# Low halves of four paired feed-forward chunks: subtracted on VectorE instead of loaded from DRAM, with a new list of order shifts

## The chip, the cores and the metric

The kernel runs on one core of a Trainium2 chip. The core has five engines that the profile names: PE (TensorE, matmul; PEld is its weight load), DVE (VectorE), ACT (ScalarE), POOL (GpSimd) and SP (SyncE, which issues nearly all DMAs here). Each engine works through its own list of instructions in order; semaphores tie the lists together. The metric is the device time of one execution in microseconds (us), as a median of several runs.

## What is computed

A transformer block on x of 2048 rows by 640 columns: layer norm, attention with 32 heads of 20 over a window of 8 keys spaced by 2, output product and residual; then layer norm and a SwiGLU feed-forward of width 1728, and residual.

```python
def _B_ref(x, w_gate, w_up, w_down):
    g = _silu(x @ w_gate)
    u = x @ w_up
    return (g * u) @ w_down

x = A_x
h = x + _A_ref(_layernorm(x, axis=-1), A_wqkv, A_wo)
h2 = h + _B_ref(_layernorm(h, axis=-1), B_w_gate, B_w_up, B_w_down)
return h2
```

All inputs and the output are float32.

## The kernel before

**Three passes for one product.** TensorE gets its operands in a reduced format (`F32R`). Each float32 operand is split into a high half (a cast, on ScalarE) and a low half (the float32 value minus the high half, a subtraction on VectorE). A product is the sum of three passes: high weights by high rows, high weights by low rows, low weights by high rows. The low half of a weight is thus wanted by the last pass only.

**Blocks and chunks.** The 2048 rows are four blocks `b` of 512. The feed-forward's width is cut into 14 chunks `i` of 128 (the last has 64). A chunk's weights are one row of `in_ffn`: 1280 columns of gate and up, 640 of down. Blocks 0 and 1 run all chunks in `ffn`. Blocks 2 and 3 share their chunks 0 to 11 in six pairs (p, p+6) by a scheme that saves one of eight products. Its first part, `early(p)` (L1074), runs chunk p with block 2 alone: two of the five column groups first, whose sums go to DRAM as `msc`, then the other three, the gate, and the first 320 columns of down. The later part is `pair(p)` (L1177). Chunks 12 and 13 run in `plain`. "The third block" is block 2; "its last four paired chunks" are `early(2)` to `early(5)`.

**How a chunk's weights come in.** `load_ffn` (L933) loads the raw chunk into one of two raw buffers in turn (L939), has ScalarE cast gate and up (L940) and down (L941) to the high halves, and then gets the low halves in one of two ways. With block 0 VectorE subtracts them (`split`, L957, in pieces of 640 columns) and SP stores them in DRAM, as `lsc`. With blocks 1 and 2 (`LOADED`, L26) SP loads them from `lsc` (L945): gate and up in one load, down in another. Chunks take turns in two buffers for gate and up (`GU`) and three for down (`DN`), so a low half can be written once the chunk two (three) back has been multiplied.

**What runs beside it.** While TensorE works on chunks 0 to 5 of block 2, the kernel also finishes attention for block 3, multiplies by `wo` for block 3 (L891) and normalises its rows, and forms combinations of down weights (`down_combinations`, L1117: loads L1121, subtractions L1124, casts L1131, low halves L1132, stores L1134 to `tsc`). When these are through, `column_combinations` (L1137) forms sums of the columns of blocks 2 and 3 (L1148 to L1165), which `pair` multiplies. The additions of L1115 move the first products of down out of four banks.

**What sets the order.** `Plan.add` notes each operation with its engine, a cost and what it reads and writes; the dependencies follow from that. `Plan.order` runs a planner over the whole list several times, with costs and due times, and gets a start for each operation. To it is added a shift from `SHIFT`, a table from the operation's number to microseconds. The program is then written in order of these sums, as far as the dependencies allow, and that order is each engine's order. `SHIFT` has 318 entries, over the whole length of the kernel. The engines' waits are put in by the dependencies, whatever the order.

Of the kernel before, what the change touches and what calls it, by code (L numbers as in the profile page):

```python
# [10 lines left out]
F32 = mybir.dt.float32  # L11
# [13 lines left out]
KEPT = range(NF)  # L25
LOADED = (1, 2)  # L26
TURN = (1,)
# [10 lines left out]
PR = {'tp': 6, 'mx': 2, 'mh': 2, 'ml': 2, 'mld': 3, 'dt': 2.2, 'g1': 0.6, 'y1': 0.6, 'x': 0.5, 'yst': 8, 'yld': 2, 'wqd': 4, 'wqh': 0.5, 'wql': 4, 'qev': 1, 'kvs': 0.4, 'atl': 1.2, 'exp': 0.5, 'ost': 3, 'wod': 2, 'woh': 8, 'wol': 1.2, 'old': 1.5, 'fld': 4, 'lst': 6, 'wev': 1.5, 'fh': 2.2, 'fl': 8, 'ln1': 8, 't1': 1, 'wo0': 1.2, 'wo': 2.2, 'ln1t': 1.2, 'xb': 0.4, 'tr': 10, 't1t': 2.2, 'ln1d': 0.5, 'hst': 10, 'hld': 10, 'ht': 1, 'hc': 2, 'jd': 3, 'jp': 8, 'js': 4, 'jl': 0.4, 'ja': 0.5, 'jfld': 1.2, 'jfh': 4, 'jfl': 1, 'jhi': 4, 'jmu': 0.4, 'jlo': 0.9, 'jcm': 0.5, 'w3': 1, 'w3e': 8, 'w3o': 0.4, 'w3x': 8, 'w3l': 2.2, 'jy': 6}  # L38

SHIFT = {  # L40
# [190 lines left out]
def program(tc, x_in, wqkv_in, wo_in, ffn_in, ffl_in, const_in, out):  # L231
# [7 lines left out]
    with tc.tile_pool(name="sb", bufs=1) as sb, tc.tile_pool(  # L239
# [89 lines left out]
        def rf(o, n):  # L329
            return ("fa", o, o + n)  # L330
# [4 lines left out]
        def rr(o, n):  # L335
            return ("ra", o, o + n)
# [596 lines left out]
        def load_ffn(b, i, gu, dn, m=640):  # L933
# [9 lines left out]
            if b in LOADED and i in KEPT:  # L943
                for o, at_, m in parts:
                    P.add("SP", 0.45, lambda o=o, at_=at_, m=m: Q.dma_start(r_(at_, m).bitcast(F32), lsc[i, :, o : o + m]), r=[(f"L{i}", o, o + m)], w=[rr(at_, m)], prio=PR["fld"], nbytes=nb(128, 4 * m))  # L945
                return
# [3 lines left out]
            split("DVE", dn[1], raw + n, dn[0], 640, 64 if last else 0)  # L950
# [3 lines left out]
        def split(eng, lo, raw, hi, n, p0):  # L954
            E, c = (V, tt(640)) if eng == "DVE" else (G, 1.8)
            for o in range(0, n, 640):
                P.add(eng, c, lambda o=o: E.tensor_sub(ra[p0:, lo + o : lo + o + 640], fa[p0:, raw + o : raw + o + 640], ra[p0:, hi + o : hi + o + 640].bitcast(F32)),  # L957
                      r=[rf(raw + o, 640), rr(hi + o, 640)], w=[rr(lo + o, 640)], prio=PR["fl"])
# [99 lines left out]
        def plain(i, x, xr):  # L1058
# [4 lines left out]
            load_ffn(2, i, gu, dn)  # L1063
# [10 lines left out]
        def early(p):  # L1074
# [4 lines left out]
            load_ffn(2, p, gu, dn, 320)  # L1079
# [442 lines left out]
```

## Time and profile before

| what | value |
| --- | --- |
| time, median of 3 runs | 838.03 us (836.65 to 838.71) |
| the profiled execution: time | 839.46 us |
| the profiled execution: span | 837.3 us |
| granted TensorE clock, mean | 0.998 |
| instructions: TensorE matmuls | 4061 |
| instructions: VectorE | 916 |
| moved by DMA | 211.08 MB |

The span runs from the first to the last instruction; the time holds a little more. A share of busy time is a mean over stages: on TensorE the kernel begins with the products for q, k and v (up to about 240 us) and goes on with the feed-forward of blocks 0 and 1 (to about 550 us), then chunks 12 and 13 and the early chunks of block 2 (to about 645 us), then the pairs, and from about 771 us the last down products. VectorE works on attention from the first stage until about 570 us. A row of the waits reads: engine and place, what it waited for, us in total, times, longest. A row of groups reads: line, engine, operation, what is written from what, shapes, count, then busy us, mean ns, and idle time before. A row of the chain or the timeline begins with the start and the length in us; SPq marks SP's queue of DMA issues.

### The profile page before, as it was taken

How to read it: one execution, taken by the hardware profiler on the slowest of the kernel's cores; microseconds unless marked ns; L12 is line 12 of the kernel's file. 1: busy time of each engine (PE TensorE's matmuls, PEld its weight loads, DVE VectorE, ACT ScalarE, POOL GpSimd, SP SyncE). 2: the span in 40 equal slices, each digit the busy share in tenths (PEclk: the TensorE clock that was granted, in tenths of full speed). 3: DMA queues.
4: the chain of work that ended last, by engine and by line, in shares of the span. 5: the costliest groups of instructions: out<-in, count | busy, mean ns of one | idle time of the engine just before them, and what ended most of it. 6: DMA issues, size and time to landing. Idle time of an engine off the chain costs nothing.

```text
span 837.3 us, 11299 instructions
## 1 busy us (share of the span) xinstructions
PE 827.1 (99%) x4061; PEld 713.5 (85%) x4061; DVE 756.1 (90%) x916; ACT 421.0 (50%) x740; POOL 23.1 (3%) x34
## 2 busy tenths in 40 slices
PE   8999999999999999999999999999999999999997
PEld 6888888889978888887888988888888888888997
DVE  7599999999999999999999999998869888777982
ACT  7856463333682435754543386565695333323440
POOL 0000000000100000001000000000000000000000
PEclk9999999999999999999999999999999999999999
DMA  8896968568679665899899668889999634357721
GB/s 274 296 363 253 284 200 275 199 201 307 185 217 351 242 192 194 313 308 352 281 319 350 250 188 317 260 267 315 375 348 312 227 115 150 128 182 250 269 105 68
DMA packets 113223, 211.08 MB, mean 252 GB/s; under 512 B 37952, under 2 KB 70400, under 8 KB 112528
## 3 DMA queue, kind: packets, MB, share of 16 engines
q1 hardware_dynamic: 113008, 210.12, 74.1%
q8 instruction: 32, 0.52, 0.3%
q10 hardware_dynamic: 160, 0.25, 0.1%
q14 instruction: 23, 0.19, 0.1%
HBM read 151.27 MB, written 59.05 MB: 251 GB/s over the span
## 4 chain that ended last, share of the span: by engine, by line
PE 86%; DVE 7%; DMA 3%; issue 2%; ACT 0%; SPq 0%; DVEq 0%; ACTq 0%
PE bank L963 22%; PE bank L644 20%; PE bank L1047 16%; PE bank L974 11%; PE bank L1299 7%; PE bank L891 4%; PE bank L1069 2%; DVE fa L693 1%; DVE fa L700 1%; DMA tsc<-acts 1%; DMA ra<-lsc 1%; PE bank L1094 1%; DVE fa L736 1%; PE bank L1104 1%; DMA fa<-in_ffn_dram 1%
## 5 line engine op out<-in xcount | busy, mean ns | idle before, releaser
L963 PE MATMUL bank<-shb,ra 128*128 128x512 f32 x810 | 190.0, 390 | 1.2 <-DVE shb L508 1.2
L963 PEld LDWEIGHTS bank<-shb,ra 128*128 128x128 f32 x810 | 151.4, 188 | 32.7 <-ACT shb L507 1.4
L644 PE MATMUL bank<-ra,sha 128*128 128x480 f32 x480 | 105.0, 379 | 0.0
L644 PE MATMUL bank<-ra,shb 128*128 128x480 f32 x470 | 102.5, 378 | 0.0
L644 PEld LDWEIGHTS bank<-ra,sha 128*128 128x128 f32 x480 | 90.2, 188 | 13.6
L644 PEld LDWEIGHTS bank<-ra,shb 128*128 128x128 f32 x470 | 88.1, 188 | 13.2
L693 DVE TENSOR_TENSOR fa<-fa 128x2560 f32<-128x2560 f32 x32 | 90.3, 2821 | 0.9 <-DMA fa<-ksc 0.2
L728 DVE TENSOR_TENSOR fa<-fa 128x2560 f32<-128x2560 f32 x32 | 90.3, 2823 | 0.8
L1047 PE MATMUL bank<-shb,ra 128*128 128x512 f32 x360 | 89.7, 395 | 0.7 <-DVE fa L991 0.6
L700 DVE TENSOR_REDUCE fa<-fa 128x128 f32<-128x2560 f32 x32 | 90.0, 2813 | 0.4
L974 PE MATMUL bank<-ra,acts 128*128 128x512 f32 x328 | 80.7, 391 | 0.0
L1047 PEld LDWEIGHTS bank<-shb,ra 128*128 128x128 f32 x360 | 65.8, 188 | 16.8 <-DVE fa L1224 1.7
L736 DVE TENSOR_TENSOR fa<-fa 128x1280 f32<-128x1280 f32 (+2 forms) x70 | 76.8, 1097 | 1.3
L649 ACT ACTIVATE st<-bank,fa 128x480 f32<-128x480 f32 x64 | 41.1, 656 | 69.7 <-PE bank L644 65.3
L891 PE MATMUL bank<-ra 128*128 128x320 f32 x480 | 74.4, 310 | 0.7 <-ACT ra L808 0.6
L891 PEld LDWEIGHTS bank<-ra 128*128 128x128 f32 x480 | 71.7, 188 | 3.7 <-ACT fa L894 1.6
L974 PEld LDWEIGHTS bank<-ra,acts 128*128 128x128 f32 x328 | 61.2, 188 | 13.2 <-DVE acts L998 0.5
L1047 PE MATMUL bank<-ra 128*128 128x512 f32 x288 | 69.1, 390 | 0.0
L1047 PEld LDWEIGHTS bank<-ra 128*128 128x128 f32 x288 | 53.9, 188 | 11.2
L1224 DVE TENSOR_TENSOR fa<-bank,fa 128x512 f32<-128x512 f32 x60 | 41.1, 690 | 19.9 <-PE bank L1047 19.1
L940 ACT CAST ra<-fa 128x1280 fp32r<-128x1280 f32 (+1 forms) x38 | 45.6, 1206 | 24.2 <-PE bank L963 12.3
L997 ACT CAST acts<-fa 128x512 fp32r<-128x512 f32 x34 | 21.0, 619 | 47.6 <-DVE fa L987 45.9
(189 smaller groups left out, 1061.8 us busy)
## 6 DMA issues: line engine op xcount, KB each, us to landing
fa<-in_ffn_dram SPq DMA_DIRECT2D x28, 960.0 KB, 6.7
fa<-ksc SPq DMA_DIRECT2D x16, 880.0 KB, 5.1
fa<-vsc SPq DMA_DIRECT2D x16, 880.0 KB, 7.6
ra<-lsc SPq DMA_DIRECT2D x21, 640.0 KB, 6.1
ra<-lsc SPq DMA_DIRECT2D x27, 320.0 KB, 3.6
lsc<-ra SPq DMA_DIRECT2D x13, 640.0 KB, 4.7
fa<-in_ffn_dram SPq DMA_DIRECT2D x12, 640.0 KB, 3.9
ra<-tsc SPq DMA_DIRECT2D x8, 960.0 KB, 7.3
```

The source lines that it names most:

```text
L644: T.matmul(banks[bk][:, 0:480], l, r_(wq(g, w, c), 480), start=(p, c) == first_mm, stop=(p, c) == last_mm)
L649: P.add("ACT", act(480) + 0.06, lambda bk=bk, j=j: A.activation(stage_t()[:, so : so + 1920].rearrange("p (t j c) -> p t j c", t=3, j=NJ)[ ...
L693: P.add("DVE", dve(2560), lambda: V.tensor_tensor(f(PROD, 2560).rearrange("p (j w c) -> p j w c", j=2, w=W), window(ko, 2 * jp), f(qo + 32 ...
L700: P.add("DVE", dve(2560), lambda: V.tensor_reduce(f(lo + 128 * jp, 128), f(PROD, 2560).rearrange("p (n d) -> p n d", d=DH), axis=AX.X, op= ...
L728: V.tensor_tensor(f(PROD, 2560).rearrange("p (j w d) -> p j w d", j=2, d=DH), bass.AP(tensor=fa[:, vo : vo + 160].tensor, offset=fa[:, vo ...
L736: V.tensor_add(dst(v), v[:, :, 0:m, :], v[:, :, m : 2 * m, :])
L891: T.matmul(banks[bk][:, 0:320], l, r_(m, 320), start=p == 0 and c == 0, stop=p == 2 and c == NC - 1)
L940: P.add("ACT", act(n), lambda: A.copy(r_(gu, n), f(raw, n)), r=[rf(raw, n)], w=[rr(gu, n)], prio=PR["fh"])
L963: T.matmul(banks[bk], r_(gu + 1280 * w + wid * c + col, 128), x2(a, c), start=p == 0 and c == 0, stop=p == 2 and c == NC - 1)
L974: T.matmul(banks[bk][:, lo:hi], l, m, start=first and p == 0, stop=last and p == len(passes) - 1)
L1047: T.matmul(banks[bk], r_(ws[w] + 256 * q, 128), x(a, c), start=start and p == n == q == 0, stop=stop and p == 2 and n == len(terms) - 1 an ...
L1299: T.matmul(banks[bks[j]][:, 0:320], t(a, 128, 128 * j), r_(ws[w], 320), start=p == q == 0, stop=p == NP - 1 and q == 2)
```

## The change

Two names are new: `MADE_EARLY`, the paired chunks whose low halves are made, and `MADE_LAST`, the same for the last chunks with block 3, which is empty. `load_ffn` takes a flag `made`, and with it goes the way of block 0, subtraction on VectorE, but stores nothing. `split` is made to take widths under 640, since an early chunk has 320 columns of down. So `early(2)` to `early(5)` lose two loads each from `lsc` (1280 and 320 columns) and gain three subtractions each (640, 640 and 320 columns). Since each such chunk has one operation more, the numbers of all later operations move up by one to four. The table `SHIFT` is replaced as a whole: 220 entries for 318, and of the operations in the one 58 are in the other too. One of the new entries names a new operation (1893, the second subtraction of chunk 2).

```diff
+MADE_EARLY = (2, 3, 4, 5)
+MADE_LAST = ()
...
-    7: 3.5, 9: -106.8, 22: 0.4, 31: -515.8, 32: -221.5, 33: -238.8, 34: -84.5, 35: -34.6, 36: -483.8, 37:
...
+    8: 4.6, 9: -130.2, 14: 2, 18: 1.5, 21: 1.1, 29: -118.6, 33: -131.6, 34: -30.4, 35: -16.7, 36: -93.7, 37:
...
+    1856: -25.6, 1857: -71.3, 1868: 1, 1872: 8.2, 1874: 2.3, 1877: 7, 1878: -75, 1879: -127.1, 1881: -31.3,
+    1882: -100.7, 1883: -151.9, 1884: -53.5, 1893: 20.6, 1898: -4.7, 1903: -0.9, 1918: 2, 1923: -54.8, 1931:
...
-        def load_ffn(b, i, gu, dn, m=640):
+        def load_ffn(b, i, gu, dn, m=640, made=False):
...
-            if b in LOADED and i in KEPT:
+            if b in LOADED and i in KEPT and not made:
                 for o, at_, m in parts:
                     P.add("SP", 0.45, lambda o=o, at_=at_, m=m: Q.dma_start(r_(at_, m).bitcast(F32), lsc[i, :, o : o + m]), r=[(f"L{i}", o, o + m)], w=[rr(at_, m)], prio=PR["fld"], nbytes=nb(128, 4 * m))
                 return
             split("DVE", gu + 1280, raw, gu, n, 0)
...
-            split("DVE", dn[1], raw + n, dn[0], 640, 64 if last else 0)
+            split("DVE", dn[1], raw + n, dn[0], m, 64 if last else 0)
...
         def split(eng, lo, raw, hi, n, p0):
-            E, c = (V, tt(640)) if eng == "DVE" else (G, 1.8)
+            E, k = V if eng == "DVE" else G, min(n, 640)
             for o in range(0, n, 640):
-                P.add(eng, c, lambda o=o: E.tensor_sub(ra[p0:, lo + o : lo + o + 640], fa[p0:, raw + o : raw + o + 640], ra[p0:, hi + o : hi + o + 640].bitcast(F32)),
-                      r=[rf(raw + o, 640), rr(hi + o, 640)], w=[rr(lo + o, 640)], prio=PR["fl"])
+                P.add(eng, tt(k) if eng == "DVE" else 1.8, lambda o=o: E.tensor_sub(ra[p0:, lo + o : lo + o + k], fa[p0:, raw + o : raw + o + k], ra[p0:, hi + o : hi + o + k].bitcast(F32)),
+                      r=[rf(raw + o, k), rr(hi + o, k)], w=[rr(lo + o, k)], prio=PR["fl"])
...
-            load_ffn(2, i, gu, dn)
+            load_ffn(2, i, gu, dn, made=x is not x2 and i in MADE_LAST)
...
-            load_ffn(2, p, gu, dn, 320)
+            load_ffn(2, p, gu, dn, 320, p in MADE_EARLY)
```

55 rows, old and new, of the table SHIFT are left out of this document.

## The prediction

> **What bounds the kernel now.** I read the page first, then the windows by stage, TensorE's waits, the stretch around the paired chunks in windows of 10 us, and the queues there.
>
> ```profile
> span 837.3 us, 11299 instructions
> ...
> PE 827.1 (99%) x4061; PEld 713.5 (85%) x4061; DVE 756.1 (90%) x916; ACT 421.0 (50%) x740; POOL 23.1 (3%) x34
> ```
>
> The profiled execution took 839.46 us, 2.16 beside its span; the median, 838.03, lies 1.43 below it. So a span S stands for a median of S + 2.16 - 1.43 = S + 0.73. TensorE is busy for all but 10.2 us of the span, and the change takes no matmul away. It can win only idle time of TensorE; these windows and waits say where that is.
>
> ```profile
> 60.00:120.00 60.00, 60.00 (x280) 52.15 (x279) 59.28 (x46) 40.38 (x82) 3.44 (x4) 1.00 0.78 255
> ...
> 180.00:240.00 60.00, 58.78 (x316) 53.27 (x315) 59.40 (x58) 34.72 (x74) 3.90 (x4) 1.00 0.70 224
> ...
> 563.00:618.00 55.00, 53.55 (x310) 47.54 (x309) 43.83 (x88) 35.77 (x66) 0.00 (x0) 1.00 0.96 343
> ...
> 760.00:838.00 78.00, 72.94 (x475) 71.02 (x473) 55.12 (x96) 26.26 (x44) 0.00 (x0) 1.00 0.46 162
> ```
>
> ```profile
> PE bank L605 <- DVE sha L608: 1.8, 1, 1.8
> PE bank L555 <- POOL ra L1401: 1.3, 1, 1.3
> PE bank L963 <- DVE shb L508: 1.2, 1, 1.2
> PE bank L891 <- ACT ra L808: 0.6, 1, 0.6
> PE bank L1047 <- DVE fa L991: 0.6, 1, 0.6
> PE bank L891 <- ACT fa L894: 0.2, 1, 0.2
> PE bank L1047 <- ACT fa L986: 0.2, 1, 0.2
> ```
>
> The columns of a window are its length, then busy time of PE, PEld, DVE, ACT and POOL, clock, DMA share and GB/s. Of the 10.2 us, 4.4 lie behind the last matmul (77.3 us from 760 to the span's end, less 72.94) and 3.1 in the two waits of the first microseconds, L555 and L605. What is left in the middle is 1.2 in 180 to 240 and 1.45 in 563 to 618, the stretch where the DMA engines are busy for 96% and where the paired chunks begin: 2.7 us in all. Those four parts make 10.2, so everywhere else TensorE runs without a break.
>
> **The change, removed.** Each of four chunks loses one load of 640 KB and one of 160 KB from the store of low halves.
>
> ```profile
> ra<-lsc SPq DMA_DIRECT2D x21, 640.0 KB, 6.1
> ...
> ra<-lsc SPq DMA_DIRECT2D x6, 160.0 KB, 4.8
> ```
>
> ```profile
> 579.23 1.07 SPq L945 DMA_DIRECT2D ra<-lsc  x2
> ...
> 630.49 0.49 SPq L945 DMA_DIRECT2D ra<-lsc  x1
> ```
>
> ```profile
>   PEld bank L1047: 0.2, 1
> ```
>
> Between the first and the last of these two issues stand nine loads; eight go (the ninth is chunk 1's down half). That is 4 x 800 KB = 3.28 MB, at the 343 GB/s of the stretch 9.6 us of full DMA. But of all low-half loads between 560 and 660 us TensorE's side waited for one, and for 0.2 us (the last row). The gain can come only by way of other transfers that run faster:
>
> ```profile
> 582.36 9.78 DMA tsc<-acts
> ...
> 593.72 1.29 DVE fa L1124 x3
> ...
> 607.12 2.12 PE bank L1047 x8
> ```
>
> In the chain the store of turned weights takes 9.78 us in the saturated stretch; its buffer, then ScalarE's and VectorE's work behind it, lead to the waits for L894 and L986 (0.15 each; rounded to 0.2 in their rows). With the first three of the removed loads gone from 579 to 591 us, these 0.3 us can go. The waits for L991 and L808 (1.15 together) end before the first removed load is issued: only the order can mend them. I take half of them, 0.6, with 0 and 1.15 as ends. Removal and order in this stretch: -0.9 (ends 0 and -1.45).
>
> **Added.** Per chunk two subtractions of 640 columns and one of 320, as in L957 (same form) and L1124 (320 columns):
>
> ```profile
> L957 DVE TENSOR_TENSOR ra<-fa,ra 128x640 fp32r<-128x640 f32 x40 | 31.8, 819 | 0.0
> ...
> L1124 DVE TENSOR_TENSOR fa<-fa 128x320 f32<-128x320 f32 x24 | 11.1, 488 | 1.9 <-DMA fa<-in_ffn_dram 1.6
> ```
>
> 8 x 0.819 + 4 x 0.488 = 8.5 us of VectorE. Back to back they overlap a little: in the chain above three L1124 take 1.29, 0.43 each instead of 0.488; 12 x 0.06 less gives 7.8. [...] I keep 8.5 as the safe end. What hides it:
>
> ```profile
> 593.00:603.00 10.00, 9.85 (x62) 9.11 (x61) 9.37 (x24) 7.74 (x14) 0.00 (x0) 1.00 1.01 375
> 603.00:613.00 10.00, 9.85 (x54) 8.18 (x53) 6.83 (x16) 8.68 (x17) 0.00 (x0) 1.00 0.96 339
> 613.00:623.00 10.00, 10.00 (x54) 8.64 (x53) 5.08 (x9) 9.49 (x16) 0.00 (x0) 1.00 0.99 347
> 623.00:633.00 10.00, 10.00 (x49) 8.21 (x49) 10.00 (x16) 7.60 (x12) 0.00 (x0) 1.00 0.98 360
> 633.00:643.00 10.00, 10.00 (x50) 8.57 (x49) 9.36 (x11) 5.75 (x8) 0.00 (x0) 1.00 0.95 315
> 643.00:653.00 10.00, 10.00 (x49) 8.41 (x48) 8.71 (x12) 5.17 (x8) 0.00 (x0) 1.00 0.88 289
> 653.00:663.00 10.00, 9.99 (x47) 8.17 (x46) 9.58 (x15) 5.27 (x10) 0.00 (x0) 1.00 0.46 160
> 663.00:673.00 10.00, 10.00 (x53) 8.73 (x52) 6.92 (x12) 1.25 (x3) 0.00 (x0) 1.00 0.62 203
> ```
>
> VectorE idles 0.63 + 3.17 + 4.92 + 0 + 0.64 = 9.4 us from 593 to 643, and 8.1 of that from 603 to 623. A subtraction can start when ScalarE has cast the high half, and is wanted by the third of a product's three passes:
>
> ```profile
> 613.33 1.27 ACT L940 CAST ra<-fa 128x1280 fp32r<-128x1280 f32 x1
> ...
> 625.77 1.26 ACT L940 CAST ra<-fa 128x1280 fp32r<-128x1280 f32 x1
> ```
>
> ```profile
> 617.57 3.66 PE L1047 MATMUL bank<-shb,ra 128*128 128x512 f32 x15
> ...
> 631.60 6.99 PE L1047 MATMUL bank<-shb,ra 128*128 128x512 f32 x30
> ```
>
> Chunk 3, cast by 614.6, is begun by TensorE at 617.6: with four matmuls of the first two passes ahead there are over 3 us, and its first subtraction takes 0.8. Chunk 5, cast by 627.0, is begun in the second half of the row at 631.6 (its first 15 matmuls end chunk 4), near 635: 8 us for 2.1 us of work. So the places suffice if the order uses them; the one shift given to a new operation (1893, chunk 2's second subtraction, +20.6) puts it off. Chunks 2 and 3 (4.3 us) fit the idle 8.1; chunks 4 and 5 push up to 4.3 us of combinations behind, into a VectorE that is full from 623 to 643. What gives way there is work that nobody needs soon:
>
> ```profile
> 648.39 3.06 DVE L1115 TENSOR_TENSOR fa<-bank,fa 128x640 f32<-128x640 f32 x4
> ```
>
> These additions only free banks that come into use again in the last products, and 663 to 673 has 3.1 us idle. I put the subtractions at nothing. If the cover is gone, chunks 4 and 5 cost 4.3 less the idle of 623 to 663 (0 + 0.64 + 1.29 + 0.42 = 2.35), so 1.9; and if all four fall into the full stretch, 8.5 - 2.35 = 6.2 us.
>
> **A wait added.** A raw buffer now stays taken until the subtractions have read it, not only until the cast:
>
> ```profile
> SPq L939 <- ACT ra L940: 3.8, 2, 2.5
> ```
>
> The raw load of the chunk after next waits some 2.1 us longer at the head of SP's queue, with the loads of L1121 and stores of L1085 and L1134 behind it; eight low-half issues are gone from that queue. Nothing of it reaches TensorE as long as raw data lands several microseconds before its cast. I take 0, ends -0.2 and +1.2 (the longest wait in the middle of TensorE's list).
>
> **The order everywhere else.** The list of shifts is another: 318 entries become 220, and 58 operations have one in both. It sets every stage. Where TensorE had no break a new order can only lose; the wait of 1.2 at 239 us can go (-1.2). For a loss the nearest row is that same wait: I take half of it, +0.6, with ends -1.2 and three such waits, +3.7.
>
> **Sum.** -0.9 + 0 + 0 + 0.6 = -0.3: a span of 837.0, a median of 837.7 us. By its ends this case runs from 836.3 to 839.5.
>
> **Rivals.** *The order mends the middle.* All 2.7 us of waits go and nothing new comes: span 834.6, time 835.3. For it: half of these waits stand in the stretch whose DMA load falls. Against: two of its four waits end before any removed load, and 1.2 us lie at 239 us.
>
> *VectorE's queue is blocked (slower).* A subtraction put ahead of a gate's product (L987) or its low half (L998), while its cast has not run, holds these; TensorE then stands for the chunk's banks. Such waits exist:
>
> ```profile
> DVE fa L987 <- ACT fa L986: 2.7, 2, 2.1
> ...
> DVE acts L998 <- ACT acts L997: 1.6, 1, 1.6
> ```
>
> The mean of L987's is 1.35; once in each of four chunks it is 5.4: span 842.7, time 843.4. It decides from the point where VectorE has no idle time left in front of the gate, as from 623 on. Against: chunks 2 to 4 can be subtracted before. [...]
>
> *The new order opens waits in other stages (slower).* Three of 1.2: span 841.0, time 841.7. For it: these stages have nothing to gain, and most shifts are new.
>
> *The change frees DMA time that nobody wanted.* Its loads were hidden and its subtractions are too: 838.0.
>
> **How the numbers follow.** A measurement of this kernel tells about 0.3%, 2.5 us, from no change. The forecast has 0.36, the last rival 0.05: both are within. The mended middle, 0.21, is faster. The blocked queue, 0.21, and waits elsewhere, 0.17, are slower. Faster 0.21, same 0.41, slower 0.38. The range takes in the mended middle with a little from the first microseconds, 834.6, and the blocked queue, 843.8.
>
> **What would show it.** VectorE's split (L957 here) x52 instead of x40, low-half loads down by eight, 3.28 MB less moved; from 593 to 643 VectorE at 48 of 50 us or more, and a DMA share near 0.8 there instead of 0.98. If I am right, TensorE's waits in 563 to 618 fall to about half and no wait over 1.3 us stands elsewhere. I am wrong if TensorE waits for L987, L957 or L998 between 608 and 660 (blocked queue), if a stage that now has 60.00 busy of 60 loses over 1 us (order), or if the wait at 239 us and those in the stretch are all gone (faster).

## The result, and the profile after

| what | value |
| --- | --- |
| time before, median of 14 runs | 838.01 us (836.00 to 839.45) |
| time after, median of 14 runs | 840.23 us (838.50 to 843.03) |
| ratio | 1.0033, 95% interval 1.0022 to 1.0044 |
| profiled execution after: time, span | 839.64 us, 837.4 us |

The changed kernel is 0.33% slower by this ratio, some 2.8 us; the two medians alone lie 2.2 us apart. The forecast was 837.7, a change that can't be told from none. The time lies inside the range of 834.6 to 843.8, but on the other side of 838, and by more than the measurement's uncertainty. The profiled execution of before was one of its slower ones (839.46 against a median of 838.01), that of after one of its faster ones (839.64 against 840.23), so the two spans, 837.3 and 837.4, hide what the medians show. The stages have to be compared with more traces than these two; the table at the end of this section does that.

The page of after (head, DMA total, one of the DMA issues):

```profile
span 837.4 us, 11310 instructions
...
PE 826.3 (99%) x4061; PEld 714.5 (85%) x4061; DVE 761.2 (91%) x928; ACT 426.6 (51%) x742; POOL 23.4 (3%) x34
...
DMA packets 112072, 207.81 MB, mean 248 GB/s; under 512 B 37824, under 2 KB 69760, under 8 KB 111376
...
ra<-lsc SPq DMA_DIRECT2D x17, 640.0 KB, 5.2
```

The change does what it says: four large loads from `lsc` fewer (21 to 17), 3.27 MB less moved (211.08 to 207.81), twelve more instructions on VectorE (916 to 928), 5.1 us more of its time. All lines of after stand nine above those of before, because the table is shorter: `split` is L948 there, the product of the early chunks L1038, that of `plain` L1060.

The waits of TensorE in after (engine and place, what it waited for, us, times, longest):

```profile
PE bank L1038 <- DMA ra<-lsc: 1.7, 1, 1.7
PE bank L546 <- POOL ra L1392: 1.3, 1, 1.3
PE bank L635 <- ACT ra L609: 1.2, 1, 1.2
PE bank L596 <- ACT fa L384: 1.0, 1, 1.0
PE bank L1060 <- ACT fa L977: 0.9, 1, 0.9
PE bank L954 <- ACT shb L498: 0.7, 1, 0.7
```

Three of the rows (L546, L635, L596) are the first microseconds. Before, the list had no wait for a load; now the longest of all is one, for the low half of chunk 0, which is still loaded. No row waits for a half that is made. The wait at 239 us (L954, L963 of before) went from 1.2 to 0.7, with no help of the change: runs below that keep the old order there show 0.7 too.

The stretch for which the prediction named numbers, after, in windows of 10 us (length, then busy PE, PEld, DVE, ACT, POOL, clock, DMA share, GB/s):

```profile
593.00:603.00 10.00, 10.00 (x62) 9.39 (x61) 9.83 (x23) 6.00 (x11) 0.00 (x0) 1.00 0.99 363
603.00:613.00 10.00, 10.00 (x57) 8.74 (x57) 7.46 (x21) 9.59 (x19) 0.00 (x0) 1.00 0.93 354
613.00:623.00 10.00, 10.00 (x53) 8.37 (x52) 8.14 (x14) 9.94 (x17) 0.00 (x0) 1.00 0.73 243
623.00:633.00 10.00, 10.00 (x50) 8.58 (x49) 9.96 (x16) 7.07 (x11) 0.00 (x0) 1.00 0.93 323
633.00:643.00 10.00, 9.83 (x48) 8.05 (x46) 9.93 (x12) 4.64 (x7) 0.00 (x0) 1.00 0.92 324
```

VectorE is busy for 45.3 of the 50 us, where it was 40.6; the prediction's sign was 48 or more. TensorE loses 0.17 us here, less than before (0.30). So up to 643 us the place where the work was added pays nothing. A wait of 0.88 us that begins at 642.8 us (L1060 in the list, for the silu of a gate on ScalarE) lies mostly behind these windows; what holds that silu is open. Two long windows show where else it is paid. Before:

```profile
60.00:540.00 480.00, 478.74 (x2276) 410.17 (x2275) 472.18 (x447) 245.58 (x419) 20.09 (x24) 1.00 0.78 262
540.00:663.00 123.00, 121.54 (x628) 104.20 (x627) 106.89 (x175) 78.33 (x133) 1.71 (x2) 1.00 0.90 312
```

After:

```profile
60.00:540.00 480.00, 479.25 (x2279) 411.61 (x2278) 469.88 (x445) 250.52 (x420) 20.43 (x24) 1.00 0.77 262
540.00:663.00 123.00, 120.38 (x631) 104.55 (x630) 112.64 (x186) 77.64 (x133) 1.72 (x2) 1.00 0.84 283
```

From 60 to 540 us only the order differs, and VectorE does the same work in both. (On ScalarE the new order brings two more loads of an activation table, 34 for 32, 1.28 us each; ScalarE is busy for 250.52 us there instead of 245.58, in mid_second below for 250.53, in mid_first for 246.32. Their cost was not tried apart.) TensorE idles 0.75 us there instead of 1.26, and other traces of the old order have 0.76 (table below), so by its own waits the new order is no worse. But VectorE idles 10.12 instead of 7.82. In this stretch VectorE is nearly as full as TensorE: a second chain with little slack, and what it loses can come due when attention ends and the kernel turns to the third block. There, from 540 to 663 us, TensorE idles 2.62 instead of 1.46.

The same windows of the other kernels of this study (idle is the length less the busy time; the kernels are explained below):

| kernel | order 60 to 540 | VectorE idle 60:540 | TensorE idle 60:540 | TensorE idle 540:663 | ratio to before |
| --- | --- | --- | --- | --- | --- |
| before | old | 7.82 | 1.26 | 1.46 | 1 |
| before_9th | old | 7.81 | 0.76 | 0.34 | 1.0002 |
| start_new | old | 8.06 | 0.76 | 0.56 | 1.0001 |
| late_new | old | 7.74 | 0.76 | 1.53 | 1.0014 |
| late_new_7th | old | 7.71 | 0.76 | 2.36 | 1.0021 |
| late_new_13 | old | 7.64 | 0.76 | 1.26 | 1.0002 |
| late_new_13_gate | old | 7.79 | 0.76 | 0.83 | 1.0002 |
| made_behind | old | 7.65 | 0.76 | 4.71 | 1.0061 |
| mid_first | new to 240 | 8.90 | 1.51 | 0.30 | 1.0015 |
| mid_second | new from 240 | 8.71 | 0.73 | 2.30 | 1.0011 |
| mid_new | new | 9.98 | 1.40 | 1.75 | 1.0019 |
| after | new | 10.12 | 0.75 | 2.62 | 1.0033 |
| start_old | new | 9.95 | 1.60 | 2.07 | 1.0030 |
| cols_early | new | 9.98 | 0.75 | 1.45 | 1.0048 |
| load_7th | new | 9.26 | 1.97 | 1.90 | 1.0042 |
| load_7th_cols | new | 10.09 | 0.73 | 2.16 | 1.0043 |
| both | new | 9.87 | 0.75 | 2.03 | 1.0050 |
| store_first | new | 10.24 | 2.16 | 3.19 | 1.0055 |

Each row is one execution; the ratio is the one on record for all runs of that kernel. VectorE's idle time follows the order in every row: 7.6 to 8.1 with the old one, 8.7 and 8.9 with half of the new one, 9.3 to 10.2 with the new one. No kernel with the new one in this stretch is under 1.0019. TensorE's own idle time up to 540 us, 0.75 in after and 0.76 in late_new_13, tells nothing of the kind. Nor does its idle time behind 540 us follow the order in every row: mid_first has the least of all, 0.30.

### The profile page after: what moved, and what is told of

Same layout as the page of the kernel before. It is cut to its first block, busy times and chain, and to the rows that moved or that the text cites. A ratio compares the mean times of both kernels' runs of the same rounds, so it can differ in the third digit from the quotient of the medians.

```text
span 837.4 us, 11310 instructions
## 1 busy us (share of the span) xinstructions
PE 826.3 (99%) x4061; PEld 714.5 (85%) x4061; DVE 761.2 (91%) x928; ACT 426.6 (51%) x742; POOL 23.4 (3%) x34
## 2 busy tenths in 40 slices
DMA packets 112072, 207.81 MB, mean 248 GB/s; under 512 B 37824, under 2 KB 69760, under 8 KB 111376
## 4 chain that ended last, share of the span: by engine, by line
PE 87%; DVE 7%; ACT 2%; DMA 2%; issue 1%; SPq 0%; DVEq 0%
PE bank L635 25%; PE bank L954 19%; PE bank L1038 14%; PE bank L965 9%; PE bank L882 8%; PE bank L1290 7%; PE bank L1095 1%; PE bank L1060 1%; DMA dsc<-fa 1%; DVE fa L719 1%; DMA fa<-in_x_dram 0%; DVE fa L727 0%; DMA ra<-lsc 0%; DVE fa L684 0%; PE bank L1085 0%
## 5 line engine op out<-in xcount | busy, mean ns | idle before, releaser
L954 PE MATMUL bank<-shb,ra 128*128 128x512 f32 x810 | 190.0, 390 | 0.8 <-ACT shb L498 0.7
L954 PEld LDWEIGHTS bank<-shb,ra 128*128 128x128 f32 x810 | 151.7, 188 | 32.2 <-ACT shb L498 1.0
L635 PE MATMUL bank<-ra,sha 128*128 128x480 f32 x480 | 106.3, 382 | 1.2 <-ACT ra L609 1.2
L635 PEld LDWEIGHTS bank<-ra,sha 128*128 128x128 f32 x480 | 91.0, 190 | 15.0 <-ACT ra L609 1.4
L635 PE MATMUL bank<-ra,shb 128*128 128x480 f32 x470 | 102.5, 379 | 0.0
L635 PEld LDWEIGHTS bank<-ra,shb 128*128 128x128 f32 x470 | 88.1, 188 | 13.2
L1038 PE MATMUL bank<-shb,ra 128*128 128x512 f32 x360 | 89.6, 394 | 1.7 <-DMA ra<-lsc 1.7
L1038 PEld LDWEIGHTS bank<-shb,ra 128*128 128x128 f32 x360 | 66.2, 188 | 16.2 <-DMA ra<-lsc 2.2
L1038 PE MATMUL bank<-ra 128*128 128x512 f32 x288 | 69.0, 391 | 0.0
L1038 PEld LDWEIGHTS bank<-ra 128*128 128x128 f32 x288 | 53.8, 188 | 11.7 <-DVE fa L1215 0.3
L948 DVE TENSOR_TENSOR ra<-fa,ra 128x640 fp32r<-128x640 f32 (+2 forms) x53 | 41.0, 794 | 3.7 <-ACT ra L932 2.5
```

The costliest lines, as they stand in the source:

```text
L635: T.matmul(banks[bk][:, 0:480], l, r_(wq(g, w, c), 480), start=(p, c) == first_mm, stop=(p, c) == last_mm)
L954: T.matmul(banks[bk], r_(gu + 1280 * w + wid * c + col, 128), x2(a, c), start=p == 0 and c == 0, stop=p == 2 and c == NC - 1)
L1038: T.matmul(banks[bk], r_(ws[w] + 256 * q, 128), x(a, c), start=start and p == n == q == 0, stop=stop and p == 2 and n == len(terms) - 1 an ...
```

## The experiments

Each ran in five rounds beside the kernel before; ratios are to before, with 95% intervals. The theories bear letters in the expectations: A, the first 20 us, in which before shows a granted TensorE clock of 0.50 from 9 to 11 us and after from 10.5 to 13, the half-clock stretch of the expectations; B, the waits of TensorE from 555 to 660 us that the trace of after shows, at 566 and 643; C, the twelve subtractions hold VectorE's queue; D, a wait at 157 us for a turned column; E, the low half of chunk 0 is issued late; G, formed from the first twelve runs, the new order costs VectorE's chain up to 540 us and, behind it, puts a product ahead of its weights. "Old" and "new" shifts are those of before and of after; "planned" is the planner's start. Lines in an experiment's rows are moved by the length of its table.

**start_old and start_new: is it the first microseconds?** The shifts of all operations planned before 60 us are exchanged.

```diff
 start_old: the changed kernel
-SHIFT = new
+SHIFT = old below 60 us, new from 60 us
 start_new: the kernel before
-SHIFT = old
+SHIFT = new below 60 us, old from 60 us
```

> The kernel after, with the shifts of every operation planned before 60 us put back to those of before. Theory A (the loss sits in the first 20 us, where the new shifts move the half-clock stretch of TensorE onto the products for q, k and v): ratio to before 1.000 or a little under, some 838 us. Theory B (the loss is the two waits that the profile after shows in 555 to 660 us, 1.7 for a low-half load and 0.9 for L977): 1.003, some 840 us.

> The kernel before, with the shifts of every operation planned before 60 us taken from after. Theory A: 1.002 to 1.003, some 840 us, with a spread from run to run like that of after (4 to 5 us) and mean clocks down to 0.994. Theory B: 1.000.

Measured: start_old 1.0030 (1.0018 to 1.0041), start_new 1.0001 (0.9989 to 1.0013). The start costs nothing; the loss stays with the rest. Theory A falls.

**made_only and order_only: the two parts of the change, with the tables as they are.**

```diff
 made_only: the changed kernel, eight loads gone, twelve subtractions
-SHIFT = new
+SHIFT = old, renumbered
 order_only: the kernel before, all halves loaded
-SHIFT = old
+SHIFT = new, renumbered
```

> The kernel after (low halves of chunks 2 to 5 subtracted) with the list of shifts of before, renumbered; the order of the new operations is then the planner's. Theory A: 1.000 if the subtractions cost nothing. Theory C (the 12 subtractions hold VectorE's queue before the gates): 1.003 or more, with waits of TensorE behind L978 or the split between 608 and 660 us.

> The kernel before (all low halves loaded) with the list of shifts of after, renumbered. Theory A: 1.003, since the start is the new one. Theory B: 1.001 to 1.003, since the late load of chunk 0's low half is in it. Theory C: 1.000.

Measured: 1.0276 (1.0254 to 1.0298) and 1.0241 (1.0219 to 1.0264). Both are far slower than either kernel, and neither says what its part costs: the planner's own starts differ from about 570 us on as soon as the loads become subtractions, and a shift is an offset from such a start. A table on the other plan gives an order that nobody chose, with waits of TensorE of up to 3.6 us in the one trace and 3.8 in the other. The runs are lost for the question; made_behind below asks it properly.

**cols_early, store_first, both, load_7th, load_7th_cols: single entries of the new table.** An earlier subtraction of a turned column (369, for the wait at 157 us); the store of attention's last sums moved ahead of the loads (910), so that chunk 0's low half stands elsewhere in SP's queue; the first load of attention's columns moved behind (2078), which makes that low half the seventh issue behind the raw load of chunk 1; and pairs of these.

```diff
 the changed kernel's SHIFT
-369: 15.7
+369: 11.6              (cols_early, both, load_7th_cols)
+910: -21.7             (store_first, both, load_7th, load_7th_cols)
+2078: 7                (load_7th, load_7th_cols)
```

> The kernel after with one shift changed (operation 369, 15.7 to 11.6): the second column group's low half of block 3's turned rows is subtracted at some 150 us beside the first, not at 156 us behind another attention step. Theory D (part of the loss is a wait of TensorE at 157 us for this subtraction, 0 to 1.7 us from run to run): 0.5 to 1 us faster than after, ratio to before 1.002, and no wait of L635 for L521 in the profile. If D is wrong: 1.003.

> The kernel after with one shift put back (operation 910, the last store of attention's output before chunk 0, -21.7 as in before), so that the load of chunk 0's low half no longer stands behind it in SP's queue. Theory E (TensorE's wait of 1.7 to 2.1 us at 566 us for that load is most of the loss): 1.2 to 1.9 us faster than after, ratio 1.0010 to 1.002, load issued near 559 us instead of 561.8. If the wait moves to the next in line: 1.003.

> The kernel after with both of these shifts. If D and E are the whole loss: ratio 0.999 to 1.001. If a third place matters (the start, or chunk 5's gate at 643 us): 1.002.

> The kernel after with two shifts as in before (910 at -21.7; 2078, the operation that before numbers 2074, at +7), so that the load of chunk 0's low half is the seventh issue of SP's queue after chunk 1's raw load, as in before, and not the ninth. Theory E (in the kernel after, the eighth issue waits until that raw load has landed, and the low half comes 2.4 us late): issued by 559.5 us, TensorE's wait at 566 us for it gone, no second half-clock stretch; 1.5 to 2.5 us faster than after, ratio 1.000 to 1.0015. If the wait is fed by something else: 1.003 or more.

> The same with operation 369 at 11.6 (the subtraction that TensorE waits for at 157 us, moved 5 us forward). D and E together: ratio 0.999 to 1.0005. E alone: like load_7th.

Measured: 1.0048 (1.0031 to 1.0064), 1.0055 (1.0038 to 1.0072), 1.0050 (1.0036 to 1.0065), 1.0042 (1.0027 to 1.0057), 1.0043 (1.0027 to 1.0059). None is better than after (1.0033), so each missed the gain that its theory named. In cols_early the wait at 157 us is indeed absent, and nothing is gained, so theory D falls: VectorE idles as long as in after (9.98). With the load as the seventh issue TensorE still waits for it: in load_7th it goes out at 559.76 us instead of 561.77, and TensorE gets it at 565.71 instead of 565.59. So E is not the cause either.

**before_9th: a later place in the queue, in the kernel before.** One load more goes ahead of chunk 0's low half. In the built program that makes it the eighth issue behind the raw load, not the ninth that the name and the expectation say.

```diff
 the kernel before's SHIFT
+1838: 1.3
```

> The kernel before with one shift added (1838 at +1.3), so that the load of chunk 0's low half is the ninth issue, not the seventh; nothing else is moved. E: issued after 561.4 us instead of 559.1, a wait of TensorE of 1 to 2.5 us near 566 us for it, ratio 1.001 to 1.003, some runs with a second half-clock stretch. If E is wrong: 1.000.

Measured: 1.0002 (0.9991 to 1.0013). No row of TensorE's waits there is for `lsc`. A later place in the queue costs before nothing: theory E falls as the main cause.

**late_new and late_new_7th: old order up to 540 us.** The loads and subtractions are those of after; the second adds the two entries of load_7th.

```diff
 the changed kernel
-SHIFT = new
+SHIFT = old below 540 us, new from 540 us
+910: -21.7, 2078: 7    (late_new_7th only)
```

> The kernel after (low halves of chunks 2 to 5 subtracted) with the shifts of before for every operation planned before 540 us, and those of after behind it: the change in its own stage alone. D says that the wait at 157 us is gone, E that the one at 566 us stays. D and E: 1.001 to 1.002. If the loss were in the stage of the change: 1.003 or more. If it were all in the earlier stages: 1.000 or less.

> Subtractions and the new order behind 540 us, the old order before that, and the load of chunk 0's low half as the seventh issue: the change in its own stage without the late load. If the subtractions cost nothing (the prediction's step): ratio 0.9985 to 1.000, better than late_new's 1.0014. If they cost something by themselves: 1.001 or more.

Measured: 1.0014 (1.0004 to 1.0025) and 1.0021 (1.0010 to 1.0032). About half of the loss goes with the new order of a stretch that the change doesn't touch otherwise (1.0033 to 1.0014, and load_7th's 1.0042 to 1.0021). The rest lies behind 540 us; the expectation of late_new_7th would put it on the subtractions, which late_new_13 below does not bear out.

**mid_new: that stretch by itself, in the kernel before.**

```diff
 the kernel before
-SHIFT = old
+SHIFT = old below 60 us, new from 60 to 540 us, old from 540 us
```

> The kernel before, all halves loaded, with the new shifts for the operations planned from 60 to 540 us alone. Theory G, first half (the new order makes VectorE's unbroken chain from 60 to 563 us end some 1.5 us later, though TensorE shows 0.6 us less waiting there): 1.0015 to 1.0025, VectorE's last big reduction (128x2560) of attention starting near 543 us instead of 541.6, and new waits of TensorE behind 540. If the order of this stretch is neutral or better, as TensorE's waits alone say: 0.999 to 1.0005, and the remaining loss is behind 540 us alone.

Measured: 1.0019 (1.0009 to 1.0030), as G had it. No weight half is made here; all of it is order. The windows of mid_new:

```profile
60.00:540.00 480.00, 478.60 (x2274) 410.12 (x2273) 470.02 (x446) 249.86 (x420) 20.38 (x24) 1.00 0.78 261
540.00:663.00 123.00, 121.25 (x632) 104.82 (x631) 108.38 (x176) 78.61 (x133) 1.72 (x2) 1.00 0.91 315
```

VectorE idles 2.2 us more than in before up to 540. The timeline gives the delay from another side: the first number is the start of the fourth and of the last of attention's 32 big reductions, in before

```profile
76.80 2.82 DVE L700 TENSOR_REDUCE fa<-fa 128x128 f32<-128x2560 f32 x1
...
541.65 2.81 DVE L700 TENSOR_REDUCE fa<-fa 128x128 f32<-128x2560 f32 x1
```

and in mid_new

```profile
77.36 2.82 DVE L693 TENSOR_REDUCE fa<-fa 128x128 f32<-128x2560 f32 x1
...
543.75 2.81 DVE L693 TENSOR_REDUCE fa<-fa 128x128 f32<-128x2560 f32 x1
```

From the one to the other before takes 464.85 us, mid_new 466.39 (after: 466.66). The 1.5 us are the size of the loss, 0.19% or 1.6 us. TensorE's list in mid_new says where it comes out:

```profile
PE bank L967 <- DVE acts L986: 1.4, 1, 1.4
PE bank L548 <- POOL ra L1394: 1.3, 1, 1.3
PE bank L956 <- ACT shb L500: 0.7, 1, 0.7
PE bank L637 <- DVE shb L523: 0.6, 1, 0.6
```

At 551 us TensorE stands 1.4 us for the low half of block 1's last gate, a subtraction in VectorE's queue that before had ready in time; at 157 us it stands 0.6.

**mid_first and mid_second: the two halves of it.**

```diff
 the kernel before's SHIFT
+new from 60 to 240 us only    (mid_first)
+new from 240 to 540 us only   (mid_second)
```

> The kernel before with the new shifts for the operations planned from 60 to 240 us alone. If VectorE's wait at 141 us carries the loss: 1.001 to 1.002, VectorE's last big reduction about 1.1 us later than in before, and the rest of the order (mid_second) below 1.0008.

> The kernel before with the new shifts for the operations planned from 240 to 540 us alone. VectorE's idle gaps of this stretch sum to 3.7 us in mid_new against 2.4 in before: if these carry the loss, 1.001 to 1.002 and the last big reduction 1.4 us later; if TensorE's 0.5 us less of waiting there counts instead, 0.999 to 1.0003.

Measured: 1.0015 (1.0003 to 1.0027) and 1.0011 (1.0000 to 1.0023). Each adds about one microsecond to VectorE's idle time (8.90 and 8.71 against 7.82), together that of mid_new. The delay between the two reductions is 1.0 us in mid_first (465.84) and 0.4 in mid_second (465.26), 1.5 in mid_new. Both halves share the loss; the intervals don't tell which has more, and no single wait carries it (for that, the second half was to stay below 1.0008). The waits of TensorE on VectorE are, in mid_first (at 156 us) and in mid_second (at 550 us, the same low half as in mid_new):

```profile
PE bank L642 <- DVE shb L528: 0.7, 1, 0.7
...
PE bank L969 <- DVE acts L988: 1.3, 1, 1.3
```

So VectorE's delay is seen to reach TensorE behind 540 us in mid_new and mid_second; in mid_first it is not, and how that loss reaches the end stays open. The 0.5 us less of waiting that TensorE shows in the second half doesn't count for the end.

**late_new_13: one entry behind 540 us.** As late_new, with the last pass of plain chunk 13 back in front of chunk 0's first product.

```diff
 late_new's SHIFT
-1814: 3.1
```

> The changed kernel, old order up to 540 us (as in late_new, 1.0014), and one new shift less behind it: the last pass of plain chunk 13 goes ahead of the first product of chunk 0 on TensorE again, as before. Theory G, second half (TensorE stands at 566 us for a low half that can't be there yet): the wait of 1.0 to 2.2 us for ra<-lsc falls below 0.5 us and the ratio to 1.0000 to 1.0008. If what is lost there comes back as another wait, as with store_first and load_7th: 1.0012 to 1.002 again.

Measured: 1.0002 (0.9992 to 1.0013). What the entry did is seen in TensorE's timeline of after (start, length; L1038 is chunk 0, L1060 chunk 13):

```profile
562.78 1.07 PE L1038 MATMUL bank<-shb,ra 128*128 128x512 f32 x4
565.59 0.73 PE L1038 MATMUL bank<-shb,ra 128*128 128x512 f32 x2 [1.75 <-DMA ra<-lsc]
566.15 1.32 PE L1060 MATMUL bank<-shb,ra 128*128 128x512 f32 x5
```

of late_new, which differs from late_new_13 in this entry alone (L1043 is chunk 0, L1065 chunk 13):

```profile
564.89 0.73 PE L1043 MATMUL bank<-shb,ra 128*128 128x512 f32 x2 [0.85 <-DMA ra<-lsc]
```

and of late_new_13:

```profile
560.22 3.56 PE L1065 MATMUL bank<-shb,ra 128*128 128x512 f32 x15
563.62 1.07 PE L1043 MATMUL bank<-shb,ra 128*128 128x512 f32 x4
565.07 0.73 PE L1043 MATMUL bank<-shb,ra 128*128 128x512 f32 x2 [0.38 <-DMA ra<-lsc]
566.48 3.71 PE L1043 MATMUL bank<-shb,ra 128*128 128x512 f32 x15 [0.68 <-ACT fa L1080]
```

In after the two last matmuls of chunk 0's first product want the low half at 563.8, and it lands at 565.6; five matmuls that were ready stand behind. With these in front, the wait is 0.38 instead of late_new's 0.85; but behind it stands a new one of 0.68 for a copy on ScalarE (L1080). From 540 to 663 us TensorE idles 1.53 and 2.36 us in the two kernels with the entry (late_new, late_new_7th), 1.26 and 0.83 in the two without (late_new_13 and the one that follows). By the ratios, 1.0014 and 1.0021 against 1.0002 twice, the entry costs some 0.15%; the medians, 838.79 and 838.87 against 838.17 and 837.94, lie only 0.8 us apart, and the intervals of single runs overlap. All counts have the same direction; the size, 0.8 to 1.3 us, is uncertain.

**late_new_13_gate: a second buffer for the gate of every other early chunk**, the order kept. (The numbers of its table are rewritten so that each engine's order stays that of late_new_13.)

```diff
-            gu, dn, ao, so = GU[m % 2], DN[m % 3], 1024 * (m % 2), SIL
+            gu, dn, ao, so = GU[m % 2], DN[m % 3], 1024 * (m % 2), (SIL, OL)[p % 2]
```

> As late_new_13, with a second buffer for the gate of every other early chunk, so that chunk 5's gate need not wait until chunk 4's product has been stored; order otherwise the same. If the wait of 0.84 us at 643 us gives back what was gained by 620 us: 0.9985 to 0.9998, a gain of about 0.8 us on late_new_13, faster than both kernels or equal to before. If that wait was covered by others (VectorE's own queue): as late_new_13, within 0.0005.

Measured: 1.0002 (0.9991 to 1.0012), as late_new_13. The wait for the gate (L1060 in the list of after, at 643 us) was gone in late_new_13 already, so the buffer had nothing to mend; whether that wait costs something where it appears wasn't tried. Of theory B the wait at 566 us is thus supported, the one at 643 is open.

**made_behind: the loads and subtractions alone, under the order of before.** The changed program, with shifts that keep every other operation in exactly the place that it had on its engine; each subtraction stands right behind its cast.

```diff
 the changed kernel
-SHIFT = new
+SHIFT[n] = start of before + old shift - start of after     for each operation that both have
+SHIFT[n] = (the same for its cast) + 0.6 or 1.3 us          for the twelve subtractions
```

> The changed kernel (eight low-half loads gone, twelve subtractions on VectorE), with every other operation of each engine in exactly the order of the kernel before; each subtraction stands right behind its cast. Theory C (the subtractions hold VectorE's queue in 580 to 645 us, and with it TensorE): 1.003 or more, and waits of TensorE on VectorE or on ra<-fa there. Theory G (the loss is the new order, not the work that it carries): 0.998 to 1.001, TensorE's losses from 540 to 660 us not above the 3.8 us of before.

Measured: 1.0061 (1.0048 to 1.0075), a median of 843.34. Theory C is right for this order with the subtractions at this place. TensorE's list (L1142 is the early chunks' product, L986 that of `wo`, L1082 the gate's product on VectorE, L1081 its silu):

```profile
PE bank L986 <- ACT fa L989: 1.8, 1, 1.8
PE bank L1142 <- DVE fa L1082: 1.7, 2, 1.4
...
PE bank L1142 <- ACT fa L1081: 0.7, 1, 0.7
```

The first wait can be followed through three queues, VectorE first (in brackets the idle time before, and who ended it):

```profile
592.89 1.56 DVE L1052 TENSOR_TENSOR ra<-fa,ra 128x640 fp32r<-128x640 f32 x2 [1.85 <-ACT ra L1035]
594.37 0.82 DVE L1227 TENSOR_TENSOR acts<-fa,acts 128x640 fp32r<-128x640 f32 x1
595.10 1.29 DVE L1219 TENSOR_TENSOR fa<-fa 128x320 f32<-128x320 f32 x3
```

then ScalarE

```profile
595.66 0.72 ACT L1226 CAST turns<-fa 128x640 fp32r<-128x640 f32 x1 [2.81 <-issue]
596.29 0.75 ACT L989 COPY fa<-bank 128x320 f32<-128x320 f32 x2
```

and TensorE

```profile
597.09 4.66 PE L986 MATMUL bank<-ra 128*128 128x320 f32 x30 [1.80 <-ACT fa L989]
```

VectorE stands 1.85 us at the head of its queue for chunk 2's cast, then makes the two halves; the combinations of L1219 start behind them, at 595.10. ScalarE's cast of their result, which by the program waits for the first of them and for a transfer, starts at 595.66, after 2.81 us without work; its row names no releaser, but the times put it right behind that first one. The copy that frees TensorE's bank is queued behind the cast, at 596.29, and TensorE stands 1.80. TensorE comes to chunk 2 only after 608 us. Two subtractions that nobody needs for over 10 us cost it more than their own 1.56 us, by standing in front.

## Why the prediction was wrong

**The step that failed is "the order everywhere else".** It said that where TensorE had no break a new order can only lose, and then priced that by TensorE's waits: +0.6 us, half of one wait. The price came from the wrong engine. The fence of windows showed VectorE at 59.28 and 59.40 of 60 us in the same rows in which TensorE was at 60.00 and 58.78, and only TensorE's column was read. The new order loses 1.6 us there: that is shown by mid_new (0.19%), which makes no half. VectorE idles 2.2 us more with it, which no list of TensorE's waits shows at its place; that this idle time is what costs is seen in the waits at 550 us of mid_new and mid_second, and not in mid_first. The wait at 239 us, the only one of TensorE in that stretch on which the term drew, shows 0.7 instead of 1.2 in runs of the old order too (start_new, before_9th). The end of +3.7 us held, and so did the rival "the new order opens waits in other stages", at 841.7 the nearest to the 840.23 measured. Its mechanism was half right: the new waits stand mostly behind 540 us.

**Behind 540 us the term was mis-sized as well.** The prediction looked for what the change frees there, not for what the new order on TensorE puts ahead of weights that can't be there: 0.8 to 1.3 us for entry 1814 (late_new and late_new_7th against late_new_13 and late_new_13_gate). With mid_new's 1.6 and the 0.2 that remain in late_new_13 this makes 2.6 to 3.1 us, against 2.8 measured; each part is uncertain by about 1 us.

**The ends of the sum.** The 836.3 to 839.5 that the prediction gives for its own case do not follow from the ends of its terms. Added up, these are -2.85 and, with the subtractions at nothing, +4.9: 835.2 to 842.9, which holds the 840.23 measured.

**Removed: -0.9 did not come.** The waits in 563 to 618 us did not fall by half: TensorE idles 1.45 there before, 1.74 in after, and late_new_13 has 1.26 in 540 to 663 against 1.46. The DMA share from 593 to 643 us fell from 0.98 to 0.90, not to 0.8. Three other traces with the old order and all loads behind 540 us have 0.30 to 0.56 in 540 to 663 (mid_first, before_9th, start_new), so most of the waits on which the term rested are not in every execution, and there was little to win. A term made of single waits of a few tenths from one trace is smaller than the spread between executions (836.0 to 839.5).

**Subtractions at nothing: right, given an order that suits them.** In late_new_13, halves made and new order from 540 us, 1.0002; VectorE takes up the work in its idle time (from 540 to 663 us it is busy for 112.52 of 123 us, TensorE for 121.74; in before 106.89 and 121.54), and no gain from the DMA time set free is seen, as one of the rivals had it. Under the old order, each behind its cast, the same twelve cost 0.61%, 5 us (made_behind). That this is near the 6.2 that the sum gave for all four chunks in a full stretch is luck: VectorE was busy for only 43.9 of the 50 us from 593 to 643 there, and what cost was the place in its queue. Other places under the old order weren't tried. The condition "the places suffice if the order uses them" is the one that decided.

**The blocked queue** did not happen in after: no wait for L987, L957 or L998 of before between 608 and 660 us (the one wait there, 0.88 at 643, is for the silu, L986). It is what made_behind shows, with waits for the gate's product as described and a time of 843.34 where the rival had 843.4. The agreement of the two is in part luck: the rival counted four waits of 1.35 for the gate's product, the trace has two of 1.7 together and others.

**The wait added at the raw buffers: 0**, as forecast; no row of TensorE's waits in after is for a raw load or its cast before 663 us.

None of the versions tried beats the kernel before; the best with made halves, late_new_13 and late_new_13_gate, can't be told from it.

## What to carry to other kernels

Where two engines are full in a stretch, as here for 478.74 and 472.18 of 480 us, a list of the first one's waits may not show what an order costs: read the idle time of both, and ask when the second one's chain ends and who takes over from it. Work that fitted into VectorE's idle time was free here only at the right place in its queue; the same twelve instructions cost nothing that could be measured in one order (1.0002) and 5 us in another (1.0061). And a table of offsets belongs to the plan on which it was searched: to test one part of such a change, keep each engine's order, not the table.

## What the runs showed of the hardware

**A wait of TensorE cost nearly twice its length in one trace, by the clock.** The same wait for chunk 0's low half, about 2 us long, in two kernels: TensorE's row and the window behind it, in `both`

```profile
566.89 0.73 PE L1037 MATMUL bank<-shb,ra 128*128 128x512 f32 x2 [2.02 <-DMA ra<-lsc]
...
565.00:575.00 10.00, 8.11 (x32) 6.74 (x33) 6.78 (x6) 3.27 (x6) 0.00 (x0) 0.83 0.87 260
```

and in late_new_7th

```profile
565.88 0.73 PE L1043 MATMUL bank<-shb,ra 128*128 128x512 f32 x2 [2.07 <-DMA ra<-lsc]
...
565.00:575.00 10.00, 9.12 (x50) 8.24 (x51) 7.32 (x10) 3.16 (x6) 0.00 (x0) 1.00 0.81 277
```

The granted clock is the third number from the end. Over those 10 us it is 0.83 in the first and 1.00 in the second. What the lower clock costs comes on top of the 2.02: the 5 and 15 matmuls behind the wait take 2.09 and 4.46 us, in late_new_7th 1.32 and 3.56, so 1.67 us more. Two other traces show a lower clock at this place: store_first behind 3.09 us of waiting (0.57 from 569 to 573 us) and load_7th_cols behind 1.93 (0.83 from 565 to 575). load_7th with 1.90 and start_old with 2.07 show 1.00. So like waits are followed by a lower clock in some traces and not in others; no run varied where the wait falls, and what decides it is open. Of the 14 runs of after, the three with a mean clock of 0.993 to 0.995 are those with spans of 840.0 to 840.3; that such a stretch of lower clock made them so fits, but no trace of them is there. The mean of the other eleven is 839.9 us, 2.1 above that of before (837.8), and that of all 14 is 2.7 above it; so by this estimate up to 0.6 us of the loss may be the clock's.

**The eighth issue behind a raw load waited for its landing, by a semaphore of the program.** SP's queue in before (start, length, line, count):

```profile
554.51 0.38 SPq L939 DMA_DIRECT2D fa<-in_ffn_dram  x1
554.99 1.32 SPq L814 DMA_DIRECT2D fa<-osc  x3
556.35 2.32 SPq L1368 DMA_DIRECT2D fa<-dsc  x3
559.13 2.12 SPq L945 DMA_DIRECT2D ra<-lsc  x1
561.43 0.56 SPq L1368 DMA_DIRECT2D fa<-dsc  x1
```

The raw load goes out at 554.51 and lands 6.9 us later, at 561.4; the eighth issue behind it goes out at 561.43. In after, where the eighth is a store (L761), the waits of SP's queue from 553 to 568 us have the row

```profile
SPq L761 <- DMA fa<-in_ffn_dram: 2.7, 2, 2.5
```

Such a row is read from semaphores: in the built program of before SP's 587 DMAs take eight semaphores in turn, and each issue first waits until the one eight places back has landed. So this is a wait that the program holds; no limit of the queue itself is shown. Chunk 0's low half (559.13) is the seventh. In after it comes behind the eighth and goes out at 561.77; before_9th, late_new_7th and load_7th show that this did not decide the time here.
